# Attention and S4D convolution on one core: 16 packed 32x32 tiles for a 16-point block stage, in float32, and loads at other places in SyncE's queue

## The chip, the cores and the metric

One NeuronCore of a Trainium2 chip runs the whole program in one launch. The metric is the device time of one execution in microseconds (us), the median of several runs. Engines are called as in the profile: PE (TensorE), DVE (VectorE), ACT (ScalarE), POOL (GpSimd) and SP (SyncE, which here only issues DMAs).

## The reference, cut to what matters

```python
def _A_ref(x, wqkv, wo):           # x (1, 2048, 640), 32 heads of 20
    q, k, v = split(x @ wqkv)
    p = _softmax(q @ k.T * 20 ** -0.5)
    return merge_heads(p @ v) @ wo

def _B_ref(u, ...):                # u (1, 2048, 640), 128 states a channel
    K = 2.0 * jnp.einsum("dn,dnl->dl", C, P).real      # one kernel of 2048 taps a channel
    y = irfft(rfft(u.T, 4096) * rfft(K, 4096))[:, :2048].T
    return y + u * D_skip

x = x + _A_ref(_layernorm(x), ...)
x = x + _B_ref(_layernorm(x), ...)
x = x + _A_ref(_layernorm(x), ...)
x = x + _B_ref(_layernorm(x), ...)
```

Everything is float32. Both attention layers have the same weights, and both convolutions the same kernels K, so K and its transform are made once, in the first half of the program.

## The kernel before, in words

The program goes through six stages: the head of attention 1 (layer norm, first projections), its loop, an output projection, convolution 1, and then head, loop, projection and convolution of the second pair.

**Attention's loop** (`attention`, L394). Heads are taken in eight groups of four (g), queries in four blocks of 512 (qb), keys in 16 tiles of 128 (kt). Each (g, qb, kt) has two *waves* j: eight packed 64x32 matmuls write scores S (L824), one ACT instruction takes the exponential of the 128x1024 tile into `pt` (L827), and after both waves eight packed float32 matmuls (L841) add to `pa`. A layer has 1024 waves, 128 a group. A planner with costs of its own (`Plan`, `slot`, `fill`) puts *jobs* between waves: the projections of later heads (`qk`, L560, packed 64x32; `vq`, L617, on the whole array), and in layer 1 also `contract` (L305), which makes the kernels K. `AHEAD` says how much work of jobs must be spent by which wave before a `contract` may go first; in layer 2 there is no `contract`. `fetch` (L605) turns a loaded weight tile `ws` (one buffer) into two f16 tiles (`make`) and issues the next load of `ws`. Projections go to DRAM (`qs`, `ks`, `qm`) and come back through SP's queue as `kop` and `qop` (`load_k`, `load_q`); for the next group this is issued at qb 3, kt 10 (L955).

**Output projection and the kernels' transform.** `out_proj` (L1092) runs over 16 row blocks, 30 matmuls `po` each. In layer 1 `ktransform` (L1029) is emitted inside its third row block, and the scheduler, which orders each engine's queue, mixes the two. For each of five tiles of 128 channels, `ktransform` loads `kl` (128x2048) from DRAM, transposes it (L1053), does a first DFT stage over 128 points with float32 matmuls (`pkx`, L1061) into `kx1`, and then eight times: four transposes (L1070, `pkt` to `kxt`), one 128x128 float32 matmul by the block diagonal matrix `f2` (L1078, `pkf`), two DVE shuffles of the result into `kn0` and `kn1`, an ACT sign (L1081), and after every second of these a DMA of each `kn` to `kha` and `khb`. Each of `kn0` and `kn1` has one buffer.

**Convolution** (`ssm`, L1128). With n from 0 to 39 (five channel tiles of eight) a step has: `stage2a`, eight f16 transposes of the high and low half of `x1` (L1173) and one ACT copy to `xt`; `stage2b`, three f16 matmuls of 512 columns by the block diagonal `f2` (L1186, high by high, low by high, high by low) into `psx`, a DVE shuffle and a DVE product by `ka`, POOL's product by `kb` and sum; `stage1` for the next channel tile (L1163, 12 f16 matmuls of 128 columns), an ACT copy to the high half and a DVE subtraction to the low one; `stage3` (L1198, float32) with two ACT copies to `v`; every second step `stage4` (L1208, eight float32 matmuls into `psy`) with a DVE sum into `x`, and in layer 1 four `bn_stats` for the next layer norm.

**PSUM** has eight banks. In projection and convolution they are shared out as X (stage 1), T (transposes), F (`psx`, `pkf`) and M, two banks each; the projection of layer 2 has X and four of M.

Of the kernel before, what the change touches and what calls it, by code (L numbers as in the profile page):

```python
# [32 lines left out]
AHEAD = ((0, 0.0), (110, 6.0), (236, 34.0), (364, 61.0), (600, 95.0), (740, 134.0))  # L33
# [51 lines left out]
def mha_s4d_kernel(ctx, tc, x_in, wqkv, wo, lar, aim, cr, ci, ldt, dsk,  # L85
                   c_e1, c_eb, c_f2, c_fa, c_sel, c_lv, c_id, c_sg, c_e16, c_f16, c_id16, out, parts="asas", general=None):
# [307 lines left out]
    def attention(x, stats):  # L394
# [162 lines left out]
        def jobs():  # L557
# [468 lines left out]
    def by_channel(x1, i2):  # L1026
        return x1[:, :, i2].rearrange("p g (s c) -> p s g c", c=4)

    def ktransform():  # L1029
# [6 lines left out]
        f2 = c1.tile([P, P], F32, name="f2")  # L1036
# [7 lines left out]
        def unit_load(b):  # L1044
            kl = c1.tile([P, L], F32, name="kl")
            sy.dma_start(kl, kd[b * P:b * P + P, :])
            ve.tensor_add(kl[:, 0:1], kl[:, 0:1], skip[:, b:b + 1])
            kt = c1.tile([P, NI, P], F32, name="ktr")
# [7 lines left out]
            x1 = c1.tile([P, 32, NI // 2, 16], F32, name="kx1")  # L1056
            for i2 in range(NI // 2):
                ps = pst("X", [P, 2, 2, P], F32, tag="X", name="pkx")
                for r in range(2):
                    for i in range(2):  # L1060
                        te.matmul(ps[:, r, i, :], e1[:, 2 * i2 + i, r, :], kt[:, 2 * i2 + i, :],  # L1061
                                  start=True, stop=True)
                (ve.tensor_copy if i2 % 2 else se.copy)(by_channel(x1, i2), ps.rearrange("p r i (g c) -> p (r i) g c", c=4))
                yield
            prev = None
            for q in range(9):
                if q < 8:
                    pt = pst("T", [P, 4, P], F32, tag="T", name="pkt")
                    for g in range(4):
                        te.transpose(pt[:, g, :], x1[:, 4 * q + g].rearrange("p i s -> p (i s)"), ident)  # L1070
                    xt = c2.tile([P, 512], F32, name="kxt")
                    se.copy(xt, pt.rearrange("p g k -> p (g k)"))
                if prev is not None:
# [3 lines left out]
                    px = pst("F", [P, 512], F32, tag="F", name="pkf")  # L1077
                    te.matmul(px, f2, prev, start=True, stop=True)  # L1078
                    for s in range(2):
                        ve.stream_shuffle(kn[s][:, (q - 1) % 2, :], px, [DUP0, DUP1][s])  # L1080
# [6 lines left out]
                yield  # L1087
        for b in range(NCT):
            yield from unit_load(b)
# [26 lines left out]
    def ssm_consts(c):  # L1116
# [3 lines left out]
        f2 = c1.tile([P, 2, P], F16, name="f2s")  # L1120
        sy.dma_start(f2, c_f16.rearrange("p (s k) -> p s k", s=2))
        id16 = c1.tile([P, P], F16, name="id16")
        sy.dma_start(id16, c_id16)
        fa = c1.tile([P, P], F32, name="fa")
        sy.dma_start(fa, c_fa)
        return e1, f2, id16, fa

    def ssm(x, uh, ul, consts, last):  # L1128
# [18 lines left out]
        e1, f2, id16, fa = consts  # L1147
        with ExitStack() as c:
# [6 lines left out]
            def stage1(b, x1, i2):  # L1155
                bs = slice(b * P, b * P + P)
                pool, tag = ("X", "X") if b or i2 % 4 < 2 else ("M", "mm")
# [7 lines left out]
                src = ps.rearrange("p r i (g c) -> p (r i) g c", c=4)  # L1165
                se.copy(by_channel(x1[0], i2), src)
                ve.tensor_sub(by_channel(x1[1], i2), src, by_channel(x1[0], i2))

            def stage2a(x1, q):
                pt = pst("T", [P, 2, 4, P], F16, tag="T", name="pst")  # L1170
                for k in range(2):
                    for g in range(4):
                        te.transpose(pt[:, k, g, :], x1[k][:, 4 * q + g].rearrange("p i s -> p (i s)"), id16)  # L1173
                xt = c2.tile([P, 2, 512], F16, name="xt")
                se.copy(xt, pt.rearrange("p k g c -> p k (g c)"))
                return xt

            def stage2b(b, q, xt):
# [5 lines left out]
                px = pst("F", [P, 512], F32, tag="F", name="psx")  # L1184
                for n, (f, k) in enumerate(((0, 0), (0, 1), (1, 0))):
                    te.matmul(px, f2[:, f, :], xt[:, k, :], start=(n == 0), stop=(n == 2))  # L1186
                t1 = c3.tile([P, 512], F32, name="t1")
                t2 = c2.tile([P, 512], F32, name="t2")
                ve.stream_shuffle(t2, px, SWAP)
                ve.tensor_mul(t1, px, ka)  # L1190
# [4 lines left out]
            def stage3(v, q, t1):  # L1195
                pv = pst("M", [P, 4, 2, NI, 4], F32, tag="mm", name="psv")
                for g in range(4):
                    te.matmul(pv[:, g].rearrange("p r i c -> p (r i c)"), t1[:, g * P:g * P + P], fa,  # L1198
                              start=True, stop=True)
                for r in range(2):  # L1200
                    se.copy(v[:, r, :, 4 * q:4 * q + 4, :], pv[:, :, r].rearrange("p g i c -> p i g c"))

            def stage4(b, v, i4):
                bs = slice(b * P, b * P + P)
                py = pst("M", [P, 4, P], F32, tag="mm", name="psy")
                for i in range(4):
                    for r in range(2):
                        te.matmul(py[:, i, :], eb[:, 4 * i4 + i, r, :],  # L1208
                                  v[:, r, 4 * i4 + i].rearrange("p g c -> p (g c)"),
# [12 lines left out]
            def new_x1():  # L1222
                return [c2.tile([P, 32, NI // 2, 16], F16, name=f"x1{k}") for k in range(2)]
# [7 lines left out]
            for n in range(NQ + 3 + 4):  # L1231
# [11 lines left out]
                if 3 <= n < NQ + 3:  # L1243
                    bb, qq = divmod(n - 3, 8)
                    if qq == 0:
                        vs[bb] = c2.tile([P, 2, NI, 32, 4], F32, name="v")
# [100 lines left out]
    def seq(x, general):  # L1347

        stats = None
        for n in range(0, len(parts), 2):  # L1350
            with ExitStack() as c:
# [31 lines left out]
                psum(c, M=2, T=2, F=2)  # L1383
# [17 lines left out]
def _constants():  # L1401
# [8 lines left out]
    e4 = np.eye(4)  # L1410
    f2 = np.zeros((2, 16, 4, 4, 2, 4, 4))
    fa = np.zeros((4, 2, 4, 4, 2, 16, 4))
    for r, o, m in ((0, 0, C), (1, 0, -S), (0, 1, S), (1, 1, C)):
        f2[r, :, :, :, o] = np.einsum("ihl,cd->ichld", m.reshape(16, 4, 4), e4)
    for s, o, m in ((0, 0, C), (1, 0, S), (0, 1, -S), (1, 1, C)):
        fa[:, s, :, :, o] = np.einsum("hli,cd->hlcid", m.reshape(4, 4, 16), e4)
    f2 = f2.reshape(2, NI // 2, 2, 4, P).transpose(1, 0, 2, 3, 4)
# [7 lines left out]
    cs = dict(c_e1=e1.reshape(P, -1), c_eb=eb.reshape(P, -1), c_f2=f2.reshape(P, P), c_sg=sg.reshape(P, 1),  # L1425
              c_fa=fa.reshape(P, -1), c_sel=sel.reshape(P, -1), c_lv=lv, c_id=np.eye(P))
    cs = {n: np.ascontiguousarray(a.astype(np.float32)) for n, a in cs.items()}
    for n, a in (("c_e16", e1), ("c_f16", f2)):
        a = a.reshape(P, -1)
        hi = a.astype(np.float16)  # L1430
        lo = (a - hi.astype(f8)).astype(np.float16)
        cs[n] = np.ascontiguousarray(np.concatenate([hi, lo], axis=1))
    cs["c_id16"] = np.eye(P, dtype=np.float16)
# [5 lines left out]
          "c_e16", "c_f16", "c_id16"]  # L1439
# [30 lines left out]
```

## Time and profile before

| | us |
|---|---|
| median of 3 runs (2713.97 to 2719.35) | 2716.5 |
| the profiled execution, its own time | 2718.84 |
| span of that execution | 2717.1 |
| attention loop 1, 115.5 to 1099.8 | 984.3 |
| projection 1 with `ktransform` from its first transpose to the convolution's first, 1140.9 to 1296.9 | 156.0 |
| convolution 1 from there, to 1433.0 | 136.1 |
| attention loop 2, 1503.5 to 2485.5 | 982.0 |
| convolution 2 with its start, 2560.0 to 2717.1 | 157.1 |

The profile is of one execution. A group's row gives its count, the time in which its engine was busy with it, the mean of one instruction in ns, and the idle time before it. A matmul's duration has the way through the array in it: successive ones overlap, so starts, not durations, tell what one costs. A float32 matmul shows as two records, a float32 transpose as one. Times in windows and timelines are us from the start of the span.

### The profile page before, as it was taken

What the parts mean: (1) busy time and instruction counts of PE and PEld (TensorE: products, weight loads), DVE (VectorE), ACT (ScalarE), POOL (GpSimd) and SP (SyncE); (2) the same over time, 40 slices, a digit from 0 to 9 for tenths busy, and PEclk for the clock granted to TensorE, in tenths of its full rate; (3) what the DMA queues carried; (4) which work ended last, traced back from release to release, by engine and by line L of the source; (5) the groups of instructions that cost most, each with busy time, mean ns of one, the idle gap of its engine ahead of it and who ended that gap; (6) DMA issues with size and microseconds to landing.
All of it is one profiled execution on the core that took longest, in us unless ns stands there. A gap on an engine that the chain in (4) does not pass through costs nothing.

```text
span 2717.1 us, 115609 instructions
## 1 busy us (share of the span) xinstructions
PE 2534.4 (93%) x50944; PEld 1445.2 (53%) x50944; DVE 1477.0 (54%) x3292; ACT 2337.4 (86%) x2762; POOL 852.6 (31%) x1282
## 2 busy tenths in 40 slices
PE   7899999999999988999999999899999998888998
PEld 3445444444444433777886445444445443335988
DVE  7777877778856970577776332232232220003865
ACT  7899999999999999455655899899999999997464
POOL 1132333333333343301670122222223223222376
PEclk9999999999999999999999999999999999999999
DMA  6522222232222232455542111111121112112365
GB/s 214 174 62 75 63 77 64 73 75 61 65 51 59 51 112 87 145 210 194 178 142 67 45 52 52 50 53 46 46 66 35 50 36 61 41 38 80 110 191 161
DMA packets 183153, 238.55 MB, mean 88 GB/s; under 512 B 42737, under 2 KB 128241, under 8 KB 180849
## 3 DMA queue, kind: packets, MB, share of 16 engines
q1 hardware_dynamic: 146304, 184.48, 21.0%
q0 software_dynamic: 36336, 46.59, 7.2%
q8 instruction: 402, 6.59, 1.0%
q14 instruction: 111, 0.90, 0.1%
HBM read 154.90 MB, written 76.03 MB: 85 GB/s over the span
## 4 chain that ended last, share of the span: by engine, by line
ACT 49%; PE 30%; issue 9%; DVE 7%; DMA 4%; POOL 1%; SPq 0%; ACTq 0%; DVEq 0%; POOLq 0%
ACT pt L77 47%; PE pa L841 5%; PE S L824 3%; PE psv L1198 3%; PE po L1104 3%; PE psy L1208 2%; PE m L578 2%; PE psx L1186 2%; PE psx L1163 2%; PE po L1098 1%; PE pst L1173 1%; PE pkf L1078 1%; DMA kop<-ks 1%; PE pv L544 1%; PE pq L730 1%
## 5 line engine op out<-in xcount | busy, mean ns | idle before, releaser
L77 ACT ACTIVATE pt<-S 128x1024 f32<-128x1024 f32 x2048 | 1922.9, 1037 | 46.7 <-PE S L824 37.1
L841 PE MATMUL pa<-pt,V 64*32 64x512 f32 x16384 | 1101.0, 590 | 0.9 <-DVE oc L77 0.8
L824 PE MATMUL S<-qop,kop 61*32 61x512 f16 x16384 | 880.4, 381 | 125.4 <-ACT pt L77 105.1
L824 PEld LDWEIGHTS <-kop 61*32 61x32 f16 x16384 | 375.1, 89 | 784.1 <-issue 660.0
L841 PEld LDWEIGHTS pa<-pt,V 64*32 64x32 f32 x16384 | 315.0, 106 | 69.9 <-DVE oc L77 6.6
L77 POOL DMA_DIRECT2D dn<-oc x256 | 126.7, 501 | 700.9 <-DVE oc L77 644.7
L77 DVE COPY oc<-pa 128x512 f32<-128x512 f32 x64 | 44.2, 690 | 312.1 <-PE pa L841 307.2
L77 DVE TENSOR_SCALAR qc<-m 128x512 f32<-128x512 f32 (+1 forms) x68 | 46.9, 689 | 296.4 <-PE m L578 296.4
L77 POOL DMA_DIRECT2D db<-dn x256 | 130.0, 513 | 111.6 <-DMA dn<-dr 107.7
L578 PE MATMUL m<-xh,wh 64*32 64x512 f16 x2560 | 146.7, 379 | 1.4 <-DVE qc L77 1.4
L578 PE MATMUL m<-xh,wl 64*32 64x512 f16 x2560 | 147.3, 378 | 0.0
L578 PE MATMUL m<-xl,wh 64*32 64x512 f16 x2560 | 145.5, 377 | 0.0
L77 POOL DMA_DIRECT2D ot<-oc x256 | 130.2, 516 | 12.7 <-issue 8.3
L578 PEld LDWEIGHTS <-wh 64*32 64x32 f16 x5120 | 92.5, 94 | 74.1 <-issue 32.6
L1191 POOL TENSOR_TENSOR t<-t,kb 128x512 f32<-128x512 f32 x80 | 102.0, 1276 | 72.3 <-DVE t L77 58.2
L77 ACT COPY xt<-pst 128x1024 f16<-128x1024 f16 x80 | 81.5, 1022 | 47.6 <-PE pst L1173 47.5
L77 POOL DMA_DIRECT2D dn<-dr x64 | 35.8, 559 | 257.5 <-DVE dr L77 237.1
L544 PEld LDWEIGHTS <-xh 128*128 128x128 f16 x960 | 79.6, 98 | 50.9 <-issue 35.6
L77 DVE TENSOR_TENSOR kb<-ktab 128x512 f32<-128x512 f32 x160 | 106.3, 682 | 0.0
L77 DVE TENSOR_SCALAR V<-m 128x160 f32<-128x160 f32 x64 | 20.7, 324 | 156.3 <-PE m L544 156.3
L77 DVE TENSOR_SCALAR dr<-dr 128x16 f32<-128x16 f32 x64 | 11.0, 171 | 171.8 <-DMA dr<-dn 171.6
L1020 POOL TENSOR_TENSOR ul<-u,uh 128x640 f16<-128x640 f32 x30 | 46.1, 1555 | 177.7 <-ACT uh L77 177.7
(269 smaller groups left out, 4045.7 us busy)
## 6 DMA issues: line engine op xcount, KB each, us to landing
ka<-kha SPq DMA_DIRECT2D x80, 256.0 KB
kb<-khb SPq DMA_DIRECT2D x80, 256.0 KB
db<-dn POOLq DMA_DIRECT2D x256, 64.0 KB, 2.7
kpw<-wd POOLq DMA_DIRECT2D x60, 192.0 KB, 4.8
qop<-qs SPq DMA_DIRECT2D x256, 40.0 KB
kop<-ks SPq DMA_DIRECT2D x128, 80.0 KB
ot<-oc POOLq DMA_DIRECT2D x256, 40.0 KB, 2.3
otl<-ot SPq DMA_DIRECT2D x32, 320.0 KB
```

Source lines behind the costliest of these rows:

```text
L77: made = f(out, *a, **k)
L544: chain(te.matmul(ps[:, :n], a_[:, ct, sl], m[:, ct, :], start=(k == 0), stop=(k == 14)))
L578: chain(te.matmul(ps[r][32 * t:32 * t + 32, :], a_[rows, ct, 32 * u:32 * u + 32], m[rows, ct, 512 * v:512 * v + 512], start=(k == 0), stop ...
L824: chain(te.matmul(S[32 * t:32 * t + 32, 512 * r:512 * r + 512], kt_[rows, kc + 32 * t:kc + 32 * t + 32], qt[rows, :], start=True, stop=Tru ...
L841: chain(te.matmul(pa[r][32 * j:32 * j + 32, :], V[rows, kt, VP * h:VP * h + 32], pts[j // 2][rows, 512 * (j % 2):512 * (j % 2) + 512], sta ...
L1020: (ve if s == NI - 1 else ge).tensor_sub(ul[:, s, :], u, uh[:, s, :])
L1104: te.matmul(pos[hf], oh[:, ct, :], m[:, ct, 320 * hf:320 * hf + 320], start=False, stop=(ct == NCT - 1 and m is wol))
L1163: te.matmul(ps[:, r, i, :], e1[:, e, s, r, :], m[:, s, bs], start=(n == 0), stop=(n == 2))
L1186: te.matmul(px, f2[:, f, :], xt[:, k, :], start=(n == 0), stop=(n == 2))
L1191: ge.tensor_mul(t2, t2, kb)
L1198: te.matmul(pv[:, g].rearrange("p r i c -> p (r i c)"), t1[:, g * P:g * P + P], fa, start=True, stop=True)
L1208: te.matmul(py[:, i, :], eb[:, 4 * i4 + i, r, :], v[:, r, 4 * i4 + i].rearrange("p g c -> p (g c)"), start=(r == 0), stop=(r == 1))
```

## The change

1. **The block stage.** `f2` becomes a 128x32 tile that holds one 32x32 matrix four times. `blocks` (new) does 16 float32 matmuls of 32x32 by 128 columns, tile (32 ch, 32 g) of the array, into a PSUM tile `px` of four banks, one bank for each ch. It takes the place of L1078 in `ktransform` and of L1186 in `ssm`; lines after it have other numbers (L1039 is its matmul).
2. **The layout.** `x1`, `kx1` and `v` have the channel's outer index c outermost, so that a step's four transposes read every 32nd element. In `ssm` `x1` is float32: no low half, so the DVE subtraction goes, the transposes are four in float32 in place of eight in f16, and `xt` is 128x512 float32. `c_f16` and `c_id16` are not loaded any more.
3. **PSUM.** Stage 1 draws on the transposes' two banks (T=2, no X), F has one buffer of four banks in place of two of one.
4. **Loads.** `kl` and `ktr` share a ring of two buffers, and the next `kl` is loaded after the transposes of the one before. `fetch` makes or loads at one call, not both (`elif`), `vq` takes its weights one step later. Loads for the next group of heads are issued at kt 8 in place of kt 10. `AHEAD` has other numbers at three points.

```diff
-AHEAD = ((0, 0.0), (110, 6.0), (236, 34.0), (364, 61.0), (600, 95.0), (740, 134.0))
+AHEAD = ((0, 0.0), (110, 6.0), (236, 32.0), (364, 59.0), (600, 95.0), (724, 134.0))
...
-                if order and (order[0][0] == "v" or not ws_):
+                elif order and (order[0][0] == "v" or not ws_):
...
             def vq(q):
+                yield 0.0, 0.0, False, ()
                 w = wv_.pop()
...
-                    if qb == 3 and kt == 10 and g + 1 < H // 4:
+                    if qb == 3 and kt == 8 and g + 1 < H // 4:
...
+    def blocks(f2, xt):
+
+        px = pst("F", [P, 4, 512], F32, tag="F", name="px")[:, :, :P]
+        for ch in range(4):
+            rows = slice(32 * ch, 32 * ch + 32)
+            for g in range(4):
+                te.matmul(px[32 * g:32 * g + 32, ch, :], f2[rows, :], xt[rows, g * P:g * P + P],
+                          start=True, stop=True, tile_position=(32 * ch, 32 * g))
+        return px
...
-                    px = pst("F", [P, 512], F32, tag="F", name="pkf")
-                    te.matmul(px, f2, prev, start=True, stop=True)
+                    px = blocks(f2, prev)
...
+            if b + 1 < NCT:
+                kls.append(load(b + 1))
...
-                src = ps.rearrange("p r i (g c) -> p (r i) g c", c=4)
-                se.copy(by_channel(x1[0], i2), src)
-                ve.tensor_sub(by_channel(x1[1], i2), src, by_channel(x1[0], i2))
+                se.copy(by_channel(x1, i2), ps.rearrange("p r i (c g) -> p (r i) c g", c=4))
...
-                pt = pst("T", [P, 2, 4, P], F16, tag="T", name="pst")
-                for k in range(2):
-                    for g in range(4):
-                        te.transpose(pt[:, k, g, :], x1[k][:, 4 * q + g].rearrange("p i s -> p (i s)"), id16)
+                pt = pst("T", [P, 4, P], F32, tag="T", name="pst")
+                for g in range(4):
+                    te.transpose(pt[:, g, :], by_group(x1, 4 * q + g), ident)
...
-                px = pst("F", [P, 512], F32, tag="F", name="psx")
-                for n, (f, k) in enumerate(((0, 0), (0, 1), (1, 0))):
-                    te.matmul(px, f2[:, f, :], xt[:, k, :], start=(n == 0), stop=(n == 2))
+                px = blocks(f2, xt)
...
-                psum(c, X=2)
+                psum(c, T=2)
...
-                    psum(c3, M=2, T=2, F=2)
+                    psum(c3, M=2, F=1)
...
-                psum(c, M=2, T=2, F=2)
+                psum(c, M=2, F=1)
```

How the instructions move shows at two places.

The first is PE's queue in the last channel tile of `ktransform`. `pkt` from `kx` are the transposes, `pkf` the block matmul, `po` the output projection. Before:

```order
L1078 MATMUL pkf<-kxt,f_26611 128x512
L1070 MATMUL pkt<-ident,kx_27401 128x128 x4
L1078 MATMUL pkf<-kxt,f_26611 128x512
L1070 MATMUL pkt<-ident,kx_27401 128x128 x8
L1104 MATMUL po<-wol,oh 128x320
L1104 MATMUL po<-woh,oh 128x320
L1070 MATMUL pkt<-ident,kx_27401 128x128 x4
L1104 MATMUL po<-wol,oh 128x320
```

After, at the same place (`px` is the block stage's result, `pkx` the first DFT stage, L1089 the transposes):

```order
L1080 MATMUL pkx<-ktr,e_26604 128x128 x19
L1039 MATMUL px<-kxt,f_26606 32x128 x16
L1080 MATMUL pkx<-ktr,e_26604 128x128 x9
L1089 MATMUL pkt<-ident,kx_27876 128x128 x8
L1039 MATMUL px<-kxt,f_26606 32x128 x16
L1089 MATMUL pkt<-ident,kx_27876 128x128 x12
L1039 MATMUL px<-kxt,f_26606 32x128 x16
L1089 MATMUL pkt<-ident,kx_27876 128x128 x4
L1039 MATMUL px<-kxt,f_26606 32x128 x16
```

Before, `po` stands between the steps up to the end (25 of its 480 matmuls come after the last `pkf`). Now all `po` stand ahead of the 25th of the 40 `blocks`, spread between the first 24, and behind that PE's queue has only the transform's own work and the first stage of the convolution.

The second is SP's queue in attention loop 2, where the loads for the third group of heads stand. `ws` is a tile of weights (128x5x160 is one for values), `qs<-qhi` writes a projection to DRAM, `kop` and `qop` read them back. Before:

```order
L77 DMA ws<-in_wqkv 128x5x128
L77 DMA ws<-in_wqkv 128x5x160
L77 DMA qs<-qhi 128x512
L77 DMA qs<-qlo 128x512
L77 DMA kop_30504<-ks 40x1x1024
L77 DMA kop_30504<-ks 20x1024
L77 DMA kop_30504<-ks 40x1x1024
```

After, there, and then 20 rows further on:

```order
L77 DMA ws<-in_wqkv 128x5x128
L77 DMA kop_31409<-ks 40x1x1024
L77 DMA kop_31409<-ks 20x1024
L77 DMA kop_31409<-ks 40x1x1024
L77 DMA kop_31409<-ks 20x1024
L77 DMA qop_31413<-qs 40x1x512
```

```order
L77 DMA qop_31415<-qm 1x512
L77 DMA qs<-qhi 128x512
L77 DMA qs<-qlo 128x512
L77 DMA ws<-in_wqkv 128x5x160
L77 DMA qs<-qhi 128x512
```

The 20 reads of `kop` and `qop` for the next group now stand ahead of the writes of `qs` and of the values' weights, which stood ahead of them before.

More of the change, by code (lines that the diff above doesn't have):

```diff
@@ L85, in mha_s4d_kernel @@
 def mha_s4d_kernel(ctx, tc, x_in, wqkv, wo, lar, aim, cr, ci, ldt, dsk,
-                   c_e1, c_eb, c_f2, c_fa, c_sel, c_lv, c_id, c_sg, c_e16, c_f16, c_id16, out, parts="asas", general=None):
+                   c_e1, c_eb, c_f2, c_fa, c_sel, c_lv, c_id, c_sg, c_e16, out, parts="asas", general=None):
     nc = tc.nc
@@ L1035, in ktransform @@
         sy.dma_start(e1, c_e1.rearrange("p (i r k) -> p i r k", i=NI, r=2))
-        f2 = c1.tile([P, P], F32, name="f2")
+        f2 = c1.tile([P, 32], F32, name="f2")
         sy.dma_start(f2, c_f2)
@@ L1055, in unit_load @@
                 yield
-            x1 = c1.tile([P, 32, NI // 2, 16], F32, name="kx1")
+            if b + 1 < NCT:
+                kls.append(load(b + 1))
+            x1 = c1.tile([P, 4, NI // 2, 4, 32], F32, name="kx1")
             for i2 in range(NI // 2):
-                ps = pst("X", [P, 2, 2, P], F32, tag="X", name="pkx")
+                ps = pst("T", [P, 2, 2, P], F32, tag="T", name="pkx")
                 for r in range(2):
@@ L1087, in unit_load @@
                 yield
+        kls = [load(0)]
         for b in range(NCT):
-            yield from unit_load(b)
+            yield from unit_load(b, kls.pop())
         c.close()
@@ L1119, in ssm_consts @@
         sy.dma_start(e1, c_e16.rearrange("p (s i r k) -> p s i r k", s=2, i=NI, r=2))
[L1120 to L1123, printed above, removed]
+        f2 = c1.tile([P, 32], F32, name="f2s")
+        sy.dma_start(f2, c_f2)
         fa = c1.tile([P, P], F32, name="fa")
         sy.dma_start(fa, c_fa)
-        return e1, f2, id16, fa
+        return e1, f2, fa
     def ssm(x, uh, ul, consts, last):
@@ L1196, in stage3 @@
                 pv = pst("M", [P, 4, 2, NI, 4], F32, tag="mm", name="psv")
-                for g in range(4):
-                    te.matmul(pv[:, g].rearrange("p r i c -> p (r i c)"), t1[:, g * P:g * P + P], fa,
+                for ch in range(4):
+                    te.matmul(pv[:, ch].rearrange("p r i g -> p (r i g)"), t1[:, ch * P:ch * P + P], fa,
                               start=True, stop=True)
                 for r in range(2):
-                    se.copy(v[:, r, :, 4 * q:4 * q + 4, :], pv[:, :, r].rearrange("p g i c -> p i g c"))
+                    se.copy(v[:, r, :, :, 4 * q:4 * q + 4], pv[:, :, r].rearrange("p c i g -> p i c g"))
             def stage4(b, v, i4):
@@ L1222, in new_x1 @@
             def new_x1():
-                return [c2.tile([P, 32, NI // 2, 16], F16, name=f"x1{k}") for k in range(2)]
+                return c2.tile([P, 4, NI // 2, 4, 32], F32, name="x1")
             x1 = new_x1()
@@ L1245, in ssm @@
                     if qq == 0:
-                        vs[bb] = c2.tile([P, 2, NI, 32, 4], F32, name="v")
+                        vs[bb] = c2.tile([P, 2, NI, 4, 32], F32, name="v")
                     stage3(vs[bb], qq, t1s.pop(n - 3))
@@ L1409, in _constants @@
     C, S = np.cos(a2), np.sin(a2)
-    e4 = np.eye(4)
-    f2 = np.zeros((2, 16, 4, 4, 2, 4, 4))
-    fa = np.zeros((4, 2, 4, 4, 2, 16, 4))
+    f2 = np.zeros((2, 16, 2, 16))
+    fa = np.zeros((4, 2, 16, 2, 16, 4))
     for r, o, m in ((0, 0, C), (1, 0, -S), (0, 1, S), (1, 1, C)):
-        f2[r, :, :, :, o] = np.einsum("ihl,cd->ichld", m.reshape(16, 4, 4), e4)
+        f2[r, :, o] = m
     for s, o, m in ((0, 0, C), (1, 0, S), (0, 1, -S), (1, 1, C)):
-        fa[:, s, :, :, o] = np.einsum("hli,cd->hlcid", m.reshape(4, 4, 16), e4)
-    f2 = f2.reshape(2, NI // 2, 2, 4, P).transpose(1, 0, 2, 3, 4)
+        for g in range(4):
+            fa[g, s, :, o, :, g] = m
+    f2 = np.tile(f2.reshape(2, NI // 2, 2, 32).transpose(1, 0, 2, 3).reshape(32, 32), (4, 1))
     sg = np.zeros((4, 2, 16, 1))
```

46 lines of the change are left out of this document (24 added, 22 removed).

## The prediction, made before the change was run

> **What bounds the kernel now.** I read the chain of work that ended last first (its engines and lines), then busy time by stage, then the waits inside the two attention loops.
>
> ```profile
> ACT 49%; PE 30%; issue 9%; DVE 7%; DMA 4%; POOL 1%; SPq 0%; ACTq 0%; DVEq 0%; POOLq 0%
> ```
>
> Half of the chain is ACT and a third PE, so there are stages of two kinds. The busy time by stretch (columns: length, busy us of PE, weight loads, DVE, ACT and POOL with instruction counts, granted clock, DMA share, GB/s) says which is which:
>
> ```profile
> core 0: us, PE busy (x) PEld busy (x) DVE busy (x) ACT busy (x) POOL busy (x), PEclk, DMA share, GB/s
> 115.50:1099.80 984.30, 936.03 (x24316) 450.36 (x24315) 712.61 (x1520) 963.78 (x1026) 319.95 (x540) 1.00 0.26 68
> 1140.90:1296.90 156.00, 148.53 (x986) 121.25 (x987) 112.44 (x298) 82.79 (x142) 12.55 (x9) 0.98 0.53 198
> 1296.90:1433.00 136.10, 134.92 (x1424) 120.33 (x1422) 97.94 (x239) 82.73 (x152) 103.52 (x91) 1.00 0.45 145
> 1503.50:2485.50 982.00, 904.90 (x20964) 426.72 (x20962) 236.20 (x454) 960.11 (x1025) 243.09 (x466) 0.99 0.17 47
> 2560.00:2717.10 157.10, 146.26 (x1541) 130.44 (x1538) 95.44 (x193) 87.73 (x163) 101.42 (x80) 0.98 0.58 182
> 1340.66:1347.87 7.21, 7.21 (x81) 6.47 (x79) 5.31 (x14) 4.39 (x8) 5.06 (x5) 1.00 0.45 145
> ```
>
> The loops are ACT's: 963.8 of 984.3 us and 960.1 of 982.0. There only the 20 us a layer in which ACT stands can be won. The transform's stage and both convolutions are PE's: 148.5 of 156.0, 134.9 of 136.1; in two steps of convolution 1 (last row) PE is busy for all of 7.21 us, and DVE, ACT and POOL have two microseconds to spare. In those stages, a shorter block on PE shortens the time, until another chain takes over.
>
> **Attention: the loads at kt 8.** What ACT waits for, in loop 1, loop 2, and a 30 us piece of loop 2 (sum, times, longest):
>
> ```profile
> ACT pt L77 <- PE S L824: 16.6, 21, 1.3
> ...
> ACT pt L77 <- PE S L824: 20.6, 11, 5.4
> ...
> ACT pt L77 <- PE S L824: 9.7, 4, 5.4
> ```
>
> Nearly half of loop 2's wait lies in that piece (1735 to 1765), where the third group of heads begins. SP's queue and ACT's timeline there:
>
> ```profile
> 1691.74 48.64 SPq L77 DMA_DIRECT2D ws<-in_wqkv  x2
> 1740.43 1.32 SPq L77 DMA_DIRECT2D qs<-qhi  x1
> 1741.80 0.43 SPq L77 DMA_DIRECT2D qs<-qlo  x1
> 1742.33 2.31 SPq L77 DMA_DIRECT2D kop<-ks  x4
> ...
> 1751.78 1.02 ACT L77 ACTIVATE pt<-S 128x1024 f32<-128x1024 f32 x1 [2.83 <-PE S L824]
> 1758.22 1.02 ACT L77 ACTIVATE pt<-S 128x1024 f32<-128x1024 f32 x1 [5.42 <-PE S L824]
> ```
>
> `kop` is issued from 1742.33 on, and the exponential that needs the loads runs at 1758.22, 5.4 us late; 2.83 us were lost at 1751.78 too. In the new order SP issues `kop` right behind the first `ws`, so the second `ws`, whose issue ends at 1740.38, and both `qs` no longer stand ahead: that is up to 1.9 us. kt 8 is two key tiles ahead of kt 10, four waves. A wave's floor is the exponential:
>
> ```profile
> L77 ACT ACTIVATE pt<-S 128x1024 f32<-128x1024 f32 x2048 | 1922.9, 1037 | 46.7 <-PE S L824 37.1
> ```
>
> 1922.9 / 2048 = 0.94 us, so the issue comes 3.8 us earlier, with 1.9 on top at this place. The half of `kop` that is overwritten has by then been read, so no new wait on its buffer. Of 9.7 us here that removes most of 3.8 + 1.9 = 5.7 (the 5.42 stall and part of the rest). Searching both loops for idle ACT time beside a group's first waves, I put 15 to 16 of the 37 us (16.6 + 20.6) down to such loads. Nothing says that all of it goes: a projection of the same group is put later by the moved loads, and `AHEAD` and `vq` shift single jobs between waves, which may make a new stall. Bounds: **-16 and +3** (a new stall of the median size seen, 1 us, at three starts of groups). I take **-12**, by 5.7 at the place above and about 1 at most of the other boundaries, which have 9 to 12 us between issue and use.
>
> **Projection 1 with the transform.** The chain of waits there, piece by piece, has what each kind costs PE (start, us, instructions):
>
> ```profile
> 1143.60 7.68 PE pkx L1061 x64
> ...
> 1154.59 0.44 PE pkt L1070 x4
> ...
> 1160.37 2.50 PE po L1104 x17
> 1162.87 1.76 PE pkf L1078 x4
> ```
>
> A `pkx` record is 0.12 us (two for a matmul), a transpose 0.11, a `po` 0.147, a `pkf` (two records) 0.88. The new block needs a price that no row shows: 16 tiles of 32x32. Nearest are the packed matmuls of attention:
>
> ```profile
> 300.07 0.42 PE L824 MATMUL S<-qop,kop 61*32 61x512 f16 x4
> 300.43 0.54 PE L315 MATMUL m<-kb,ka 128*32 128x64 f32 x24
> 300.90 0.41 PE L824 MATMUL S<-qop,kop 61*32 61x512 f16 x8
> ...
> 600.22 0.46 PE L824 MATMUL S<-qop,kop 61*32 61x512 f16 x8
> 600.44 1.09 PE L841 MATMUL pa<-pt,V 64*32 64x512 f32 x16
> ```
>
> Eight scores take 0.22 us from start to start (600.22 to 600.44), as long as one would, so tiles do run side by side, in two row groups and four column groups. From 300.07 to 300.43 is 0.36, and the 24 of L315, four abreast in six rounds, take 0.47. A round of 64 float32 columns taken as half of `pkx`'s 0.12 gives 6 x 0.056 = 0.34, so changing the tile shape costs 0.14 going in and 0.13 coming out. If all 16 tiles run side by side, a block is two records of 128 columns, 0.22, plus 0.27 for the two changes, plus a little for starts: **0.52 us**. Lower bound 0.46 (the second change hidden); upper bound 1.17, if the four row groups run one after another (8 x 0.112 + 0.27), which L841 and L824 speak against. I stay near the L824 and L315 rows.
>
> The 40 blocks then give back 40 x (0.88 - 0.52) = 14 us of PE work. But that is not what the stage gains. By the new order all `po` are gone before block 25, and the last 16 blocks (channel tiles 4 and 5) have only their own work. What they wait for is `kn`, here between two pairs:
>
> ```profile
> 1183.18 0.74 DVE L77 STREAM_SHUFFLE kn<-pkf 128x512 f32<-128x512 f32 x1
> 1186.06 0.01 DVE L77 LOAD_MASK_SELECT kn<-pkf  x1 [2.15 <-DMA kha<-kn]
> ...
> 1183.30 0.32 SPq L77 DMA_DIRECT2D kha<-kn  x1
> ...
> 1183.51 1.33 ACT L77 ACTIVATE kn<-kn,sgn 128x512 f32<-128x512 f32 x2
> ```
>
> From `kha`'s issue to the shuffle that may overwrite its `kn` is 2.76 us. With one `px`, a pair must go: shuffle to `kn1` 0.74, next block 0.52 and its start 0.15, shuffles 0.64 and 0.74, sign 0.72, DMA 2.76 (that of `khb` taken as that of `kha`): 6.3 us.
>
> PE's work before block 25 by the new order: 249 `po` x 0.147 = 36.6; 256 `pkx` records x 0.12 = 30.7; 160 transposes x 0.11 = 17.6; 24 x 0.52 = 12.5; together 97. The same sum for the stage before gives 141 of 156 us, 5.4 of the rest being the idle time at its end, so some 9 us over 40 blocks are lost in other ways: 5 for 24. I add 5 more for shuffles that are late by `kn` (a pair has 7 to 8 us of work, little above 6.3): 107. Then 8 pairs x 6.3 = 50, less the last DMA's 2.8, plus 1.5 at the change of tile; and behind the last sign ACT copies the convolution's eight results of stage 1, before hidden partly, by
>
> ```profile
> 1289.22 2.04 ACT L77 CAST x<-psx 128x512 f16<-128x512 f32 x4
> ```
>
> some 4.5 us. Together 160.5, against 156.0; the stage starts 1.6 us earlier (11 `po` fewer ahead of it). So **+3**, the 14 us given back and more. Bounds: **-5** if the pairs overlap with the first stage of tile 5 as now, **+16** if the 6.3 us rule all 20 pairs (126, plus 40 for five first stages, 3 for the start and 4.5, is 173.5, begun 1.6 earlier). The next `kl` is issued where it was, behind the transposes; I cost it at nothing: its 4.3 us of waits stay, PE has `po` then. Without that cover it is 2 us a tile.
>
> **The two convolutions.** The two steps of the last row of the table, on PE:
>
> ```profile
> 1340.66 1.95 PE L1208 MATMUL psy<-v,eb 128*128 128x128 f32 x16
> ...
> 1342.45 0.61 PE L1173 MATMUL pst<-id,x 128*128 128x128 f16 x8
> ...
> 1342.89 0.81 PE L1186 MATMUL psx<-xt,f2s 128*128 128x512 f16 x3
> ```
>
> By starts, stage 4 is 1.79, transposes 0.44, block 0.65 (stage 1 starts at 1343.54). Four float32 transposes cost 4 x 0.11 = 0.44, the same; they read every 32nd element now, bounded by nothing and 0.05 a step (the strided ones of L1053 last 288 ns on the mean against 276). The block goes from 0.65 to 0.52, 0.13 a step, 80 steps: -10.4. The subtraction on DVE goes, which bounds nothing here (5.31 of 7.21 us). `px` now has one buffer, so a block waits for the shuffle and product of the last:
>
> ```profile
> 1344.16 0.73 DVE L77 STREAM_SHUFFLE t<-psx 128x512 f32<-128x512 f32 x1
> ...
> 1344.79 0.68 DVE L77 TENSOR_TENSOR t<-psx,ka 128x512 f32<-128x512 f32 x1
> ```
>
> The two need 1.31 us, and where DVE first has stage 4's sum and `bn_stats` (0.69 + 0.87), 2.87; PE has about 3.0 of other work between two blocks. So it just fits, except in the last channel tile, without stage 1: +2 in all. Behind a waiting block PE's whole queue stands. Stage 1 and the transposes share two banks, each freed by an ACT copy of 0.6 us; a step has 3.5. Sum: **-9**, bounds -13 (block of 0.46) and +2 (block of 0.60 and strided reads: -4 + 4 + 2).
>
> **Sum.** -12 + 3 - 9 = -18: 2718.8 to 2700.8 for the profiled execution, which lies 2.3 above the median: 2698.5.
>
> **Rivals.**
> - *The row groups don't overlap* (slower). No row has four row groups at once. At 1.17 us a block, 80 steps lose 0.52 each (+42 in place of -9), and the transform 0.65 in 24 blocks and in one of each of the last 8 pairs (+21): +54, about 2770. It decides from 0.68 us on: 0.1 us a block is 8 + 3 = 11 us, and 18 are to be lost. Against it: eight tiles in the time of one. Chance 0.12.
> The Trainium skill's page "TensorE: Matmul & The Clock Gate" (section "Wait — 56ns, not 53.3ns?") says that matmuls never start closer than about 25 ns however few columns they have; by that, an estimate for 32 starts is 0.8 us, a block about 1.07, and the time some 2758. The rows disagree: L315's 24 records take 0.47 us with the changes of shape in them, 20 ns each.
> - *The earlier loads give nothing*: the wait is for the projection itself, or returns a wave later. For it: not every stall has SP's queue behind it. -2 in place of -12: 2708.5. Chance 0.12.
> - *`kn` rules the whole transform*: +16 in place of +3, as `po` is spread thin: 2711.5. Chance 0.12; with the one before, 2721.5, 0.04.
> - *Everything overlaps better*: blocks of 0.46, the pairs hidden: -16 - 5 - 13 gives 2682.5. Chance 0.10.
>
> **How the numbers follow.** The forecast has 0.50, with 2686 to 2711 as its own range. 0.2%, 5.4 us, is about what a measurement of this kernel can tell from no change: 2711 to 2722 count as the same. Faster: 0.50, 0.10 of the best case, 0.10 of the rival with loads and 0.03 of that with `kn`, which lies on the edge: 0.73. Same: 0.02 + 0.09 of these two, and 0.02 of both at once: 0.13. Slower: 0.12 + 0.02 = 0.14. The range leaves out the first rival and the edge of the best case: 2680 to 2724.
>
> **What would show it.** The changed kernel's profile should have 16 `px` pairs of records within about 0.5 us, two steps of convolution 1 in some 6.95 us, ACT's waits for S in the two loops down from 37 to about 25, and in the transform's last third a stretch of some 50 us in which PE is busy for about half, DVE waiting for `kha` and `khb`. Blocks above 0.68 us, ACT's waits unchanged, or a transform stage of 170 us would each make the prediction wrong.

## The result: 0.7% slower, and the profile after

The changed kernel took 2736.55 us (median of 4 runs, 2733.51 to 2740.58), the kernel before 2717.23 beside it (2713.97 to 2719.35): a ratio of 1.0073, 95% interval 1.0055 to 1.0091. The forecast was 2698.5. The profiled execution has 2740.58 us and a span of 2738.6, against 2718.84 and 2717.1 before. Here are its busy times by stretch, in the order of the table in the prediction (columns as there; the last row is again two steps of convolution 1):

```profile
core 0: us, PE busy (x) PEld busy (x) DVE busy (x) ACT busy (x) POOL busy (x), PEclk, DMA share, GB/s
117.50:1104.40 986.90, 938.29 (x24316) 451.78 (x24315) 711.02 (x1520) 963.36 (x1025) 321.99 (x541) 1.00 0.27 69
1142.05:1334.45 192.40, 152.98 (x2187) 125.69 (x2185) 111.23 (x294) 84.02 (x141) 13.33 (x10) 0.87 0.44 160
1334.45:1476.20 141.75, 137.07 (x2464) 122.88 (x2464) 83.49 (x233) 66.94 (x155) 105.11 (x93) 1.00 0.44 142
1540.20:2510.10 969.90, 900.66 (x20964) 425.76 (x20962) 236.67 (x454) 960.27 (x1025) 242.41 (x466) 1.00 0.17 48
2591.70:2738.60 146.90, 137.48 (x2464) 123.28 (x2464) 67.14 (x141) 65.90 (x152) 99.98 (x79) 0.97 0.59 184
1372.50:1379.53 7.03, 7.03 (x131) 6.38 (x130) 4.11 (x11) 3.54 (x8) 5.08 (x5) 1.00 0.48 152
```

One stage holds the loss: projection 1 with the transform has 192.4 us against 156.0, and in it PE is busy for only 153.0, at a mean granted clock of 0.87. Between fixed points (the first and last exponential of a loop, the transform's first transpose, the first transpose and the last stage 4 of a convolution), the span's 21.5 us come about as follows:

| from, to | before | after |
|---|---|---|
| start to loop 1 | 115.5 | 117.5 |
| loop 1 | 983.2 | 985.8 |
| to the transform's first transpose | 42.2 | 38.7 |
| projection 1 with the transform | 156.0 | 192.4 |
| convolution 1 to its last stage 4 | 139.7 | 140.3 |
| to loop 2 | 66.8 | 65.4 |
| loop 2 | 980.9 | 968.8 |
| from there to the end | 232.6 | 229.6 |

So the moved loads gave the 12 us of the forecast in loop 2, the convolutions gave less than the 9 of the forecast, and the transform cost 36 in place of 3. The waits of PE in the transform's stage of the changed kernel (sum, times, longest) name what was late:

```profile
PE px L1039 <- DVE kn L77: 15.6, 11, 4.5
PE pkt L1089 <- ACT kxt L77: 7.3, 12, 0.9
```

A block waits for DVE to have read the `px` before it. In the kernel before this wait was next to nothing in that stage:

```profile
PE pkf L1078 <- DVE kn L77: 0.2, 1, 0.2
```

The chain of waits shows why DVE was late (start, us, what; the last two pairs of channel tile 5):

```profile
1304.12 2.62 DMA khb<-kn
...
1306.86 0.74 DVE kn L77
...
1307.73 0.88 PE px L1039 x32
...
1308.65 1.39 DVE kn L77 x3
...
1310.06 0.73 ACT kn L77
1310.81 2.62 DMA khb<-kn
...
1313.55 0.74 DVE kn L77
...
1314.42 0.89 PE px L1039 x32
```

It is a closed cycle: DMA of `kn1`, shuffle into `kn1`, block, two shuffles, sign, DMA. From 1306.86 to 1313.55 it takes 6.69 us. In the chain of the kernel before there is no DMA of `kn`. In its last channel tile PE's own rows follow each other, up to 1274.83, from where rows of DVE have the chain:

```profile
1264.99 0.92 PE pkf L1078 x2
...
1269.03 1.03 PE po L1104 x7
...
1271.63 1.72 PE pkf L1078 x4
```

The cycle is not only in the last tiles. These are the first blocks of channel tiles 1 to 5, on PE's timeline after,

```profile
1155.38 0.40 PE L1039 MATMUL px<-kxt,f 32*32 32x128 f32 x16
...
1190.30 0.39 PE L1039 MATMUL px<-kxt,f 32*32 32x128 f32 x14
...
1225.47 0.40 PE L1039 MATMUL px<-kxt,f 32*32 32x128 f32 x16
...
1261.60 0.38 PE L1039 MATMUL px<-kxt,f 32*32 32x128 f32 x13
...
1298.74 0.40 PE L1039 MATMUL px<-kxt,f 32*32 32x128 f32 x15 [0.22 <-ACT kxt L77]
```

and before:

```profile
1153.47 0.70 PE L1078 MATMUL pkf<-kxt,f 128*128 128x512 f32 x1
...
1180.07 0.70 PE L1078 MATMUL pkf<-kxt,f 128*128 128x512 f32 x1
...
1207.25 0.70 PE L1078 MATMUL pkf<-kxt,f 128*128 128x512 f32 x1
...
1235.33 0.70 PE L1078 MATMUL pkf<-kxt,f 128*128 128x512 f32 x1
...
1262.13 0.70 PE L1078 MATMUL pkf<-kxt,f 128*128 128x512 f32 x1
```

A channel tile takes 34.9 to 37.1 us in place of 26.6 to 28.1, from the first one on, while `po` still stood between the blocks. The eight blocks of a tile spread over 28.3 to 33.4 us in tiles 1 to 4 (16 to 17 before), and 2.7 to 6.7 us follow to the next tile's first block (9.6 to 12.2 before). From one pair to the next it is 4.9 to 8.9 us at a tile's start and 6.7 to 10.0 after that, against the bare cycle's 6.7; in PE's queue `po` and parts of the next tile's first stage stand between the blocks there. How much of the excess is theirs was not taken apart.

The theory from here on (theory 1): one buffer of `px` ties the four shuffles of a pair to the order `kn0`, `kn1`, `kn0`, `kn1`, so that the second block waits for the DMA of `kn1`; this cycle sets the stage. The shuffles' waits in the traces have that order: in the changed kernel the second shuffle of a pair (1191.65, behind the first at 1191.00) waits for the DMA to `khb`; before, it is the third one (1187.81, behind two at 1186.09 and 1186.73). The rivals: the two PSUM banks that `pkx` and the transposes now share (theory 2), the halved clock, and the 16 tiles themselves.

### The profile page after: what moved, and what is told of

Same layout as the page of the kernel before. It is cut to its first block, busy times and chain, and to the rows that moved or that the text cites. A ratio compares the mean times of both kernels' runs of the same rounds, so it can differ in the third digit from the quotient of the medians.

```text
span 2738.6 us, 121989 instructions
## 1 busy us (share of the span) xinstructions
PE 2529.5 (92%) x54144; PEld 1444.5 (53%) x54144; DVE 1428.9 (52%) x3212; ACT 2305.2 (84%) x2762; POOL 854.8 (31%) x1282
## 4 chain that ended last, share of the span: by engine, by line
ACT 51%; PE 26%; issue 9%; DVE 8%; DMA 5%; POOL 0%; SPq 0%; ACTq 0%; DVEq 0%; POOLq 0%
ACT pt L77 48%; PE pa L842 4%; PE psv L1210 3%; PE S L825 3%; PE psy L1220 2%; PE po L1123 2%; PE psx L1180 2%; PE m L578 2%; PE px L1039 2%; DMA khb<-kn 1%; PE pkx L1080 1%; PE pst L1187 1%; DMA kop<-ks 1%; PE pq L731 1%; DVE kn L77 1%
## 5 line engine op out<-in xcount | busy, mean ns | idle before, releaser
L77 ACT ACTIVATE pt<-S 128x1024 f32<-128x1024 f32 x2048 | 1922.7, 1037 | 37.2 <-PE S L825 28.1
L1204 POOL TENSOR_TENSOR t<-t,t 128x512 f32<-128x512 f32 x78 | 99.7, 1278 | 6.1
L315 PEld LDWEIGHTS m<-kb,ka 128*32 128x32 f32 x3840 | 61.0, 109 | 72.2 <-issue 54.8
L1123 PE MATMUL po<-wol,oh 128*128 128x320 f32 x320 | 96.4, 314 | 0.0
```

The lines of the kernel that those rows point to most:

```text
L77: made = f(out, *a, **k)
L315: chain(te.matmul(ps[32 * j:32 * j + 32, c8, :], a[n][:, ch, :], b[n][:, dd, :], start=(n == 0), stop=(n == 2), tile_position=(0, 32 * j)))
L1123: te.matmul(pos[hf], oh[:, ct, :], m[:, ct, 320 * hf:320 * hf + 320], start=False, stop=(ct == NCT - 1 and m is wol))
L1204: (ge if g0 else ve).tensor_add(t1, t1, t2)
```

## The experiments

Each was timed in alternation with the kernel before; that one's median was 2721.34 us beside the first four kernels, 2721.27 beside the next four, 2718.77 beside the last three. "Stage" is the time from the transform's first transpose to the convolution's first, in the profiled execution.

**One number of the kernel before** (e5). This was run after e1 to e4, but it carries the verdict.

```diff
-                    psum(c3, M=2, T=2, F=2)
+                    psum(c3, M=2, T=2, F=1)
```

> The kernel before with one number changed: one PSUM buffer in place of two for pkf in projection 1 (no tiles of 32x32, no other layout, X and T as before). Theory 1 (the cycle of kn behind a single buffer): the stage goes from 156 us to 185 to 200, po is used up near block 24 of 40, the granted clock falls at the end, and the kernel takes about 30 us more, 2747 to 2755. If the 16 tiles, their layout or the shared banks made the stage long: within 5 us of the kernel before.

Measured: 2755.91 us, ratio 1.013 (1.0113 to 1.0147), stage 189.4 us. With no tile of 32x32 in it, with `pkx` and the transposes in banks of their own, the kernel before lost 33.4 us of its stage by one buffer, and the changed kernel 36.4. PE's queue was written in the same way too: in both all 480 `po` stand ahead of block 24. The chain of waits has the same cycle:

```profile
1307.19 2.62 DMA khb<-kn
...
1309.94 0.74 DVE kn L77
...
1310.72 2.09 PE pkf L1078 x2
...
1312.84 1.36 DVE kn L77 x3
...
1314.22 0.73 ACT kn L77
1314.97 2.65 DMA khb<-kn
```

From DMA to DMA it is 7.78 us here, with a block of 2.09 us. The block is dearer than the changed kernel's, and the stage no longer: the cycle, not PE's price of a block, is what the two have in common.

**The cycle opened at `kn`** (e1).

```diff
-                    if q % 2:
-                        kn = [c1.tile([P, 2, 512], F32, name=f"kn{s}") for s in range(2)]
+                    kn = [c3.tile([P, 512], F32, name=f"kn{s}") for s in range(2)]
...
-                    if q % 2 == 0:
-                        for s, dst in enumerate((kha, khb)):
-                            sy.dma_start(dst[:, g0 - 4:g0 + 4, :].rearrange("p g k -> p (g k)"),
-                                         kn[s].rearrange("p q k -> p (q k)"))
+                    for s, dst in enumerate((kha, khb)):
+                        sy.dma_start(dst[:, g0:g0 + 4, :].rearrange("p g k -> p (g k)"), kn[s])
```

> The changed kernel with kn0 and kn1 made for each step (128x512, three buffers each) in place of one buffer for two steps, and one kha and one khb DMA a step. Theory 1 (the cycle of kn behind a single px sets the transform's stage: about 6.7 us a pair, and after it nothing hides the first stage of the next tile): without the cycle the stage of 192.4 us falls to what PE has to do, 150 to 160, po reaches to the end, the granted clock stays at 1.0, and the kernel takes about 2700 us. Theory 2 (pkx and the transposes share two PSUM banks, so the first stages are slow): the stage stays above 175 us and the kernel above 2718.

Measured: 2708.64 us, ratio 0.9948 (0.9932 to 0.9965); stage 164.2. With the single `px` kept, 28 of the 36 us are back. PE's waits in that stage:

```profile
PE psx L1178 <- ACT x L77: 8.4, 1, 8.4
PE pkx L1081 <- DVE kx L77: 3.8, 4, 1.5
PE px L1039 <- DVE kn L77: 1.9, 4, 0.6
```

A block's wait for DVE is down from 15.6 to 1.9 us. The stage is above the 150 to 160 that I expected. At its end, the convolution's first copy to `x1` waits for the last DMA of `kn`, and PE for that copy (8.4 us). From the chain, DMA, copy and stage 1 in a row:

```profile
1290.56 4.90 DMA khb<-kn
1295.77 0.59 ACT x L77
...
1296.40 4.21 PE psx L1178 x48
```

The changed kernel has this tail too (DMA at 1325.59, copy at 1328.46, first transpose at 1334.45). That `x1` lies in memory which `kn` leaves is my reading of the wait; no run moved it. It is not what e1 has more than the kernel before, though: from tile 5's first block to the stage's end e1 takes 32.0 us, against 34.8 before. The excess is in the four distances between the tiles' first blocks, 118.9 us in all against 108.7. Some 5 us of that may be the shared banks (the four distances are 112.7 in e2, 117.6 in e3, below); the rest stays open.

**The cycle opened at `px`** (e2, e3). The whole-array matmul by a block diagonal 128x128 matrix comes back in `ktransform` only; the transposes pick the rows so that its output lies as that of `blocks`.

```diff
-                    px = blocks(f2, prev)
+                    px = pst("F", [P, 4, P], F32, tag="F", name="pkf")
+                    te.matmul(px.rearrange("p c k -> p (c k)"), f2, prev, start=True, stop=True)
...
-                    psum(c3, M=2, F=1)
+                    psum(c3, M=2, F=2, X=2)
```

> The changed kernel, with ktransform's block stage as one 128x128 float32 matmul by the block diagonal matrix again, in two one-bank buffers, and pkx in two banks of its own; the convolutions keep the 16 tiles. Theory 1: with two buffers DVE fills kn0 for both steps before kn1, a pair takes about 4.85 us again, and the stage is 154 to 160 us though each block costs PE 0.3 us more: about 2700 us. A theory that the stage was long for PE's own work on blocks would expect it no shorter than 192.

> As the run with two one-bank buffers in ktransform, but with pkx and the transposes in the two banks that they share in the changed kernel. Theory 1: the stage is within 4 us of the run with banks of its own for pkx. Theory 2: it is longer by 15 us or more.

Measured: e2 2703.6 us, ratio 0.9937 (0.9915 to 0.9959), stage 160.6; e3, with `F=2` alone and no X, 2711.59, ratio 0.9959 (0.9945 to 0.9973), stage 165.8. Two buffers undo most of the loss, though a block costs PE more again. The shared banks cost 5.2 us of stage in these two executions (that of e3 was its slowest of seven, 2718.51), and the ratios' intervals overlap; e5 has the loss without sharing. Theory 2 is not the cause, at most a small part.

**Both** (e8).

> The changed kernel with both mends of the transform: one whole-array matmul in two buffers with pkx in banks of its own, and kn of one step in three buffers. By its order po is left for the end. Theory 1: nothing in the stage waits for kn, PE has about 150 us of work and the stage takes 150 to 156 us, 5 to 10 less than with the first mend alone: about 2696. If kn no longer matters once there are two buffers: 160 us, about 2703.

Measured: 2704.92 us, ratio 0.994 (0.9923 to 0.9957), stage 157.8. That is not faster than with one mend. Either opening does. The second one did speed up the chain: a tile's eight blocks lie within 10.7 us, against some 16 in e2, and 169 of the 480 `po` are left behind the last block, against 25. But the stage is by then mostly PE's own work: PE is busy for 148.8 of the 157.8 us.

**The clock** (e6). The granted clock of the changed kernel is in the first three rows (the figure before the DMA share); the last two of these stretches, with matmuls added, are in the next fence.

```diff
+                    if b >= 3:
+                        dm = pst("T", [P, 512], F32, tag="T", name="dm")
+                        for _ in range(2):
+                            te.matmul(dm, ident, prev, start=True, stop=True)
```

> The changed kernel, with two matmuls more (128x512 float32, results never read) behind each of the last 16 blocks of ktransform, so that PE stands less there. If the halved granted clock at the end of the stage costs much (four transposes took 1.13 us there against 0.44): the clock stays at 1.0 and the stage is 5 to 10 us shorter than 192.4, about 2728. If the cycle of kn sets the pace whatever the clock: the same or up to 10 us longer.

```profile
1140.00:1250.00 110.00, 103.04 (x1377) 87.57 (x1375) 77.68 (x204) 52.59 (x90) 15.38 (x11) 1.00 0.42 150
1250.00:1290.00 40.00, 28.03 (x394) 21.50 (x393) 18.43 (x52) 14.40 (x24) 0.00 (x0) 0.70 0.50 185
1290.00:1310.00 20.00, 13.21 (x235) 10.32 (x233) 10.27 (x28) 8.59 (x14) 0.00 (x0) 0.89 0.26 107
```

```profile
1250.00:1290.00 40.00, 37.09 (x463) 24.01 (x463) 21.76 (x58) 16.06 (x26) 0.00 (x0) 0.97 0.46 173
1290.00:1310.00 20.00, 18.31 (x225) 10.27 (x224) 7.26 (x22) 7.48 (x12) 0.00 (x0) 1.00 0.26 106
```

Measured: 2739.09 us, ratio 1.0067 (1.005 to 1.0084), stage 193.5. The clock was held at 0.97 and 1.00 up to 1310 (0.83 from there to 1330, against 0.50), and the stage did not get shorter. The added matmuls take PE time of their own, so a gain of a few microseconds from the clock may be hidden in this. What is excluded is that the clock explains the loss: of the 36 us, 24 had come by the end of the third tile (106.2 us for three tiles, against 81.9), and up to 1250 the changed kernel's clock was 1.00.

**The moved loads alone, and in halves** (e4, e7, e9), on the kernel before.

```diff
-                if order and (order[0][0] == "v" or not ws_):
+                elif order and (order[0][0] == "v" or not ws_):
...
             def vq(q):
+                yield 0.0, 0.0, False, ()
...
-                    if qb == 3 and kt == 10 and g + 1 < H // 4:
+                    if qb == 3 and kt == 8 and g + 1 < H // 4:
```

e4 has all of it with `AHEAD`, e7 only the last line, e9 all but the last line; the three edits of e9 were not parted.

> The kernel before, with the moved loads alone: kt 8, make or load at one call, vq a step later, and the three numbers of AHEAD. If the changes of loop 1 and loop 2 in the changed kernel (+2.6 and -12.1 us) come from these alone: about 2707 us. If loop 2 gained for another reason (its SP queue stood differently after the shorter list of constants): 2714 to 2717.

> The kernel before with kt 8 in place of kt 10 alone. If the earlier issue of kop and qop is what shortens loop 2: loop 2 is 9 to 12 us shorter and the kernel about 2707. If it takes the weights' loads moved out of SP's way too (make or load, and vq a step later): 2 to 5 us, about 2714.

> The kernel before with the other half of the moved loads: make or load at one call, vq a step later, the three numbers of AHEAD, and kt 10 kept. If the two halves work by themselves (kt 8 alone took 4 us off loop 2, all together 12): loop 2 is 6 to 9 us shorter and the kernel about 2713. If the weights' loads out of SP's way help only when kop is issued earlier too: 0 to 3 us, about 2719.

Measured: e4 2706.18 us, ratio 0.9942 (0.9921 to 0.9962), loop 2 969.0; e7 2714.06, ratio 0.997 (0.996 to 0.998), loop 2 976.9; e9 2705.78, ratio 0.9957 (0.994 to 0.9973), loop 2 968.9. Both cases expected for e9 missed: it gave 12.1 us of loop 2, all that e4 gave. So the 12 us come from the weights' loads, with kt 10 as it was; kt 8 alone gave 4.0, and beside the other edits nothing. With kt 8 alone, the place of the prediction looks almost as before. SP's queue and ACT's timeline of e7:

```profile
1692.74 48.63 SPq L77 DMA_DIRECT2D ws<-in_wqkv  x2
1741.47 2.30 SPq L77 DMA_DIRECT2D kop<-ks  x4
```

```profile
1757.03 1.02 ACT L77 ACTIVATE pt<-S 128x1024 f32<-128x1024 f32 x1 [5.04 <-PE S L824]
```

And SP's queue of e9, at the same place:

```profile
1689.44 0.41 SPq L77 DMA_DIRECT2D ws<-in_wqkv  x1
1729.95 2.31 SPq L77 DMA_DIRECT2D kop<-ks  x4
```

In e7 the second `ws` holds SP's queue for 48 us, until the first is used up (43.5 us of it are a wait for DVE's `wl`, made from the first), and `kop` stands behind it however early it is asked for: it goes out at 1741.47, and ACT stands 5.04 us at 1757. In e9 the second load is no longer asked for there, and `kop` goes out at 1729.95, 17.0 us before the group starts; SP's wait ahead of it is now one of 40.0 us for PE's `S`, which reads the half of `kop` that is to be overwritten. In e4 and in the changed kernel, with kt 8, it is 17.0 us too: the buffer sets the time, and that is why kt 8 adds nothing there. In e9 between 1735 and 1766 no wait of ACT over 0.56 us is left.

**Two tries for a faster kernel** (e10, e11).

> The kernel before with all moved loads and kn of one step in three buffers (whole-array block, two pkf buffers, the convolutions as before). If PE's own work (148.5 of 156 us) sets the stage once the cycle of kn is gone: a stage of 148 to 152 us, 3 to 5 us less than the moved loads alone, about 2702. If two buffers of pkf were enough: as the moved loads alone, about 2706.

> The changed kernel with one whole-array matmul in two buffers, pkx in its own banks, and the three numbers of AHEAD of the kernel before. If these numbers made loop 1 2 us longer: loop 1 is 983 us and the kernel about 2702 on a chip where the kernel before takes 2721. If not: loop 1 stays at 985 to 986 and the kernel at 2704.

Measured: e10 (the edit of e1 on e4) 2703.12 us, ratio 0.994 (0.9922 to 0.9958), stage 154.7 against e4's 154.4: in the kernel before, `kn` set nothing that PE's work did not. Its chain too got shorter (a tile's eight blocks within 10.8 us, against 16 to 17 in e4, and 172 `po` behind the last one), with PE busy for 151.0 us of the 154.7. e11 2702.12, ratio 0.9945 (0.9926 to 0.9964), loop 1 984.0 against e2's 985.0; a difference of 1 us between single executions says nothing on `AHEAD`. Why loop 1 had 2.6 us more in the changed kernel stays open too; with the same loop, e6 has 982.1 us and e3 987.5, so single executions differ by more than that. e2, e4, e8, e10 and e11 all beat both kernels by 15 us and more, and their intervals don't tell them apart.

## Why the prediction was wrong, point by point

- **Transform (+3 forecast, +36.4 measured): the failed step.** I put block 25 at 107 us: PE's work before it (97), 5 for other losses and 5 "for shuffles that are late by `kn`". It came after 119.6 (1261.60 less 1142.05). From there to the end I had 53.5 us, and it took 72.8. I had the cycle right (6.3 us a pair against 6.69), and let it rule only where `po` had run out. It ruled from tile 1 on: with the cycle open, in e1, the first three tiles take 91.3 us in place of 106.2. A pair's PE work "little above 6.3" was no cover; as I read it, what a cycle delays in one pair is not given back by filler in the next. In the last two tiles I had written 1.5 us for the change of tile, as if the first stage lay beside the pairs, and taken off the last DMA: tile 4 took 37.1 us where that gives 26.7, and from tile 5's first block to the end it was 35.7 in place of 26.9, with the last DMA, the copy and stage 1 behind it in the chain. My rival on `kn` let the cycle rule all 20 pairs, and still fell 19 us short at 173.5: the four distances between tiles sum to 143.4 where it has 132.8 (four pairs of 6.3 and a first stage of 8 each), the end is 35.7 in place of 29.7, and the start 13.3 in place of 11.
- The reading behind it: 148.5 busy of 156 us, so PE is the bound. e10 bears that out for the kernel before, but it said nothing of how near the cycle was: `po` is filler that is placed wherever the transform leaves room, and with it spread to the end the two come out alike. The order that I had printed, with `po` gone by block 25, was the sign that the spaces between the blocks had grown, by about a third, from the first tile on.
- **The block on PE was priced well.** Forecast 0.52 us, "within about 0.5". In convolution 1 (PE's timeline):

```profile
1372.71 0.60 PE L1187 MATMUL pst<-ident,x 128*128 128x128 f32 x4
1373.25 0.50 PE L1039 MATMUL px<-xt,f2s 32*32 32x128 f32 x32
1373.68 0.23 PE L1180 MATMUL psx<-uh,e1s 128*128 128x128 f16 x1
```

  Four transposes and a block take 0.97 us from start to start; without the transposes' 0.44, the block is 0.53, changes of shape included. The rival of row groups in turn (1.17 us) is excluded. The Trainium skill's floor of about 25 ns between starts (page "TensorE: Matmul & The Clock Gate", section "Wait — 56ns, not 53.3ns?") does not hold for these tiles abreast. The row has 32 starts, and the next instruction starts 0.43 us after the first, 13 ns a start; inside each half of 16, the trace's records start 6.7 ns apart.
- **Convolutions (-9 forecast).** Two steps take 7.03 us in convolution 1, against 7.21 and the 6.95 expected. The mechanism was right where a step has stage 1 in it. In the last channel tile, without stage 1, the cheaper block gave nothing in convolution 2 (5.77 for two steps, against 5.76), and in convolution 1, where DVE also has `bn_stats`, the single `px` cost more than its +2: two steps take 6.18 against 5.76, and PE waited for DVE (the first row is convolution 1, the second convolution 2, which has no `bn_stats`):

```profile
PE px L1039 <- DVE t L77: 2.2, 5, 0.6
...
PE px L1039 <- DVE t L77: 0.2, 1, 0.2
```

  So convolution 1 kept nothing (+0.6): its three middle tiles gained 2.3 us, its last tile with the end lost 2.3, and its first lost 0.7, which stays open. From loop 2 to the end the kernel gained 3.0 us; the executions with the changed convolution have 226.4 to 229.6 us there, those with the old one 231.5 to 233.1.
- **Attention (-12 forecast).** All of it came in loop 2, where ACT's wait for S fell from 20.6 to 8.5 us; loop 1, for which I had counted a share, gained nothing (+2.6, and +0.1 in e4). The size was right in part by luck, and half of the reason was wrong. In loop 2, after:

```profile
ACT pt L77 <- PE S L825: 8.5, 8, 4.1
```

  I divided 5.7 us at the worst place into 3.8 for the four waves of kt 8 and 1.9 for the queue. e7 shows that kt 8 brings `kop` ahead of the two `qs` (1.8 us, counted from the loop's start) and no more; e9 shows that the 48 us of the queue are nearly everything. I read where the second `ws` *ended* (1740.38) and counted only what stood between that and `kop`, not the time that it stood at the queue's head.
- The "slower" that came was not the slower rival that I had worked out, but a stronger form of the rival on `kn`.

## What to carry to other kernels

Ask of a stage that looks full whether its work is a chain with filler: take the distance between equal steps of the chain (here the first blocks of five tiles) and divide it among the links of a cycle, before counting busy time. When a change takes a double buffer away, write the cycle through the single one with its DMA and all, and let it run from the first step. A DMA that waits at the head of an in-order queue costs its followers the time it waits (48 us here), so an earlier request behind it does not go out before it.

## What the runs showed of the hardware

Sixteen 32x32 tiles in float32 do run abreast: 16 matmuls of 128 columns take 0.53 us between whole-array matmuls, where one 128x128 matmul over 512 columns takes 0.88. In the trace's records of the block at 1373.25 the first pass of all 16 starts within 0.10 us, and one of them lasts 0.29. And the granted clock fell to about 0.50 in stretches in which PE was busy for about half or less (9.3 of 20 us from 1310 to 1330 in e5, at 0.51; 7.0 of 20 in the changed kernel, at 0.50), but with the clock held higher by matmuls of no use (e6) the same stage took as long, 193.5 us against 192.4: the clock was not the cause of the waiting.
